# A longer chain of reciprocals, a fourth x buffer and moved transposes in a fused attention and MoE kernel

## The chip, the cores and the metric

The kernel runs on one core of one Trainium2 chip. The metric is the device time of one execution in microseconds (us); lower is better. Engines are called by the profile's names: PE is TensorE, DVE is VectorE, ACT is ScalarE, POOL is GpSimd, and SP is the engine whose queue issues the DMAs here.

## What is computed

The reference first computes a linear attention with random features and then a gated two-layer network on its output:

```python
def phi(x):                                    # x: 8 batches, 8 heads, 576 tokens, 64 wide
    proj = einsum('bhsd,df->bhsf', x, w_phi)   # 128 features
    proj = proj - max(abs(proj), axis=-1, keepdims=True)
    return concatenate([exp(proj), exp(-proj)], axis=-1)
q_p, k_p = phi(q), phi(k)
kv  = einsum('bhsf,bhsd->bhfd', k_p, v)
z   = sum(k_p, axis=2)
num = einsum('bhsf,bhfd->bhsd', q_p, kv)
den = einsum('bhsf,bhf->bhs', q_p, z)[..., None] + 1e-6
x   = (num / den).transpose(0, 2, 1, 3).reshape(4608, 512)
out = ((x @ w_a) * (x @ w_b)) @ w_out          # 512 -> 1536 -> 512
```

## The kernel before

**The attention runs in turns.** The 64 heads are handled as 32 pairs (4 pairs to a batch); pair i starts at turn 4i. A pair's steps are spread over fixed turns: `project` (q and k through `w_phi`, products `pq` and `pk`) at turn 0 of the pair, then `kv_products`, `z_products`, `kv_out` (a copy of `kv` out of PSUM), `turned_kv` (three transposes `pt` on PE, copied to `kvh` by DVE, line 274), and `num_products` (`pn`) and `den_products` (`pd`), which both need `kvh`. The table SPREAD says which turn for the first nine pairs, and PACKED for the rest; in PACKED `turned_kv` stands at turn 5, `num_products` at 7. `attention_steps` (lines 329 to 370) collects all the steps, sorts them by turn and by a fixed order inside a turn, and issues them so. The order of PE's products is fixed by that: helper `mm`, line 105, chains each to the one before. The other engines' queues are in order too; a scheduler fills them, with lists (`marks`, `acts`, `loads`) that pin some steps behind others.

**The division runs as a chain through DRAM** (`reciprocals`, lines 305 to 327), because a denominator is needed along another axis than the one it comes out of PSUM on. It has seven steps: store `den` (line 310), load it as `r` (line 313), one reciprocal on DVE (line 315), store `rec` (line 317), load it spread over the rows as `rb` (line 321, two DMAs), multiply `x` by `rb` on DVE (line 324), store `xnorm` (line 326). Each step has a turn of its own after `den_products`: REC_TURNS0 = (1, 3, 5, 6, 8, 10, 10) for pairs 0 to 4, REC_TURNS1 = (1, 3, 4, 5, 7, 8, 8) for pairs 5 and 6, REC_TURNS = (0, 1, 3, 4, 5, 6, 6) for pairs 7 to 31. All the DMAs of the chain go through SP's queue, with the loads of k, q, v and the weights.

**The network runs beside it.** Until turn 40 the attention is alone on PE, while ACT and DVE decode the network's weights (`load_weights`, lines 424 to 436, 0.8 steps a turn from turn 3, 2.2 a turn from turn 40). From turn 41 on, blocks of the network (`moe_block`, 384 tokens, six pairs of products `pa` and `pb`, then four `po`) run in between, 0.36 steps a turn for 20 turns and 0.82 a turn afterwards (line 912). The first pass covers half of the 1536 columns; `second_pass` covers the other half after the attention.

**PSUM.** Up to turn 40 the attention has all eight banks. Afterwards `ps_moe` has three banks (tag `moe`) in which `pa`, `pb`, `po`, and also `pt` and `pd`, take turns; `ps_att` has two places of two banks (tag `att`) for `pq`, `pk` and `pn`, and one bank for `kv`.

**SBUF of the chain.** `x32` (what `pn` is copied into, line 287) has three buffers, `rb` has two.

Of the kernel before, what the change touches and what calls it, by code (L numbers as in the profile page):

```python
# [9 lines left out]
F32 = mybir.dt.float32  # L10
# [8 lines left out]
P = 128  # L19
# [2 lines left out]

TURNS, ALONE, SUM_FROM = 4, 9, 15
SPREAD = dict(turned_kv=9, kv_products=5, num_products=10, z_products=6, kv_out=6, den_products=11)
PACKED = dict(summed=2, turned_kv=5, kv_products=3, num_products=7, z_products=3, kv_out=3, den_products=7)
REC_TURNS0, REC_TURNS1, REC_TURNS, X_TURNS = (1, 3, 5, 6, 8, 10, 10), (1, 3, 4, 5, 7, 8, 8), (0, 1, 3, 4, 5, 6, 6), (5, 8)
EARLY_X = (0, 2, 4)
DECODE_TURN, BLOCK_LAG = 3, 1
DECODE_ALONE, DECODE_BESIDE = 0.8, 2.2
PACE0, PACE, PACE0_TURNS = 0.36, 0.82, 21  # L30

# [13 lines left out]
def tile_kernel(ctx, tc, qP, km, kr, vm, vr, w_phi, eye, w_a, w_b, w_out, out):  # L45
# [14 lines left out]
    B, NPAIR, _, S = qP.shape  # L60
# [43 lines left out]
    def mm(out, w, x, start=True, stop=True):  # L104
        issue = lambda: nc.tensor.matmul(out, w, x, start=start, stop=stop, skip_group_check=True)  # L105
        return pe(issue) if alone else issue()
# [3 lines left out]
    def duo(name):  # L110
        if "ps" in alone:
            return alone["ps"].tile([P, 2, 512], F32, tag=f"duo{next(duos) % 3}", name=name)
        return alone["att"].tile([P, 2, 512], F32, tag="att", name=name)

    def bank(tag, name):
        if "ps" in alone:
            return alone["ps"].tile([P, 3, P], F32, tag=tag, name=name)
        if tag == "kv":
            return alone["att"].tile([P, 3, P], F32, tag="kv", bufs=1, name=name)
        return pools_moe[0].tile([P, 3, P], F32, tag="moe", name=name)  # L120

    def attention_consts(a1):
# [116 lines left out]
    def kv_products(b, pr, a1, a2, consts, st):  # L239
        e, er = st["e", b, pr], st["er", b, pr // 2]  # L240
        v32, rv = st["v", b, pr], st["rv", b, pr // 2]
        kv = st["kv", b, pr] = bank("kv", f"kv_{b}_{pr}")
        kvs = kv.rearrange("p s f -> p (s f)")
        for c in range(NFULL):
            for j in range(2):
                mm(kvs[heads[j], : 2 * F], v32[:, c, j], e[:, j, c].rearrange("p s f -> p (s f)"), start=(c == 0), stop=False)
        for j in range(2):
            mm(kvs[heads[j], : 2 * F], rv[:, pr % 2, j], er[:, j, 0].rearrange("p s f -> p (s f)"), start=False)
# [19 lines left out]
    def turned_kv(b, pr, a1, a2, consts, st):  # L268
        u = f"{b}_{pr}"
        pt = bank("pt", f"pt_{u}")  # L270
        for g in range(3):
            pe(lambda: nc.tensor.transpose(pt[:, g], st["back", b, pr][:, g], consts[1]))
        kvh = st["kvh", b, pr] = a2.tile([P, 3, P], F32, tag="kvh", bufs=1, name=f"kvh_{u}")
        nc.vector.tensor_copy(kvh, pt)  # L274

    def num_products(b, pr, a1, a2, consts, st):
        u = f"{b}_{pr}"
        kvh, eq = st["kvh", b, pr], st["eq", b, pr]
        pn = duo(f"pn_{u}")
        for t in range(2):  # L280
            for s in range(2):
                for j in range(2):
                    mm(pn[heads[j], t, :HALF], kvh[:, s, heads[j]], eq[:, j, s, times[t]], start=(s == 0), stop=(s == 1))
        i = b * NPAIR + pr
        place, bufs = (alone["early"], 2) if i in EARLY_X else (a2, 3)
        x32 = st["x", b, pr] = place.tile([P, S], F32, tag="x32", bufs=bufs, name=f"x32_{u}")
        nc.scalar.copy(x32.rearrange("p (t n) -> p t n", t=2), pn[:, :, :HALF])

    def den_products(b, pr, a1, a2, consts, st):
        u = f"{b}_{pr}"  # L290
        kvh, eq = st["kvh", b, pr], st["eq", b, pr]
        pd = bank("pt", f"pd_{u}").rearrange("p s f -> p (s f)")
        for s in range(2):
            for j in range(2):
                for t in range(2):
                    mm(pd[strips[2 * j + t], :HALF], kvh[:, 2, strips[2 * j + s]], eq[:, j, s, times[t]], start=(s == 0), stop=(s == 1))
        dn = st["dn", b, pr] = a2.tile([P, HALF], F32, tag="dn", name=f"dn_{u}")
        nc.scalar.activation(dn, pd[:, :HALF], AF.Identity, bias=consts[3])

    def behind(what, issue):  # L300

        with tc.issue_after(what[-1].ins):
            issue()

    def reciprocals(b, pr, a1, a2, st):

        n = 2 * S // P
        hs, rows = slice(2 * pr, 2 * pr + 2), slice(pr * P, (pr + 1) * P)
        one = st["dn", b, pr].rearrange("(g r) n -> g r n", r=P // 4)[:, 0]
        behind(loads, lambda: nc.sync.dma_start(den[b][hs].rearrange("h (t n) -> (h t) n", t=2), one))  # L310
        yield
        r = a2.tile([P, n], F32, tag="rec", name=f"r_{b}_{pr}")
        behind(loads, lambda: nc.sync.dma_start(r, den[b][hs].rearrange("h (a n) -> (h a) n", n=n)))
        yield
        behind(marks, lambda: nc.vector.reciprocal(r, r))
        yield
        behind(loads, lambda: nc.sync.dma_start(rec[b][hs].rearrange("h (a n) -> (h a) n", n=n), r))
        yield
        rb = a2.tile([P, S], F32, tag="rb", name=f"rb_{b}_{pr}")
        for j in range(2):  # L320
            behind(loads, lambda: nc.sync.dma_start(rb[heads[j]], rec[b][2 * pr + j : 2 * pr + j + 1].broadcast_to([D, S])))
        yield
        x32 = st["x", b, pr]
        behind(marks, lambda: nc.vector.tensor_tensor(x32, x32, rb, op=ALU.mult))
        yield
        behind(loads, lambda: nc.sync.dma_start(xnorm[b][rows], x32))
        yield

    def attention_steps(pools, consts, st):

        stages, x_first = [], first_block_x()

        def once(f, *args):
            f(*args)
            yield

        def plan(order, unit, turns):
            for t in turns:
                stages.append((t, order, len(stages), unit))

        for i in range(B * NPAIR):
            b, pr = divmod(i, NPAIR)
            t0 = TURNS * i
            args = (b, pr, *pools, consts, st)
            at = SPREAD if i < ALONE else PACKED
            if i == ALONE - 1:
                at = dict(SPREAD, turned_kv=8, num_products=8, den_products=8)
            elif i == ALONE:
                at = dict(PACKED, kv_products=4, z_products=4, kv_out=4)
            units = ((project, 0), (q_features, TURNS), (turned_kv, 0), (summed, 0), (kv_products, 0), (num_products, 0), (z_products, 0), (kv_out, 0))  # L350
            units += ((den_products, 0), (load_kq, -5), (load_v, -2 if i else 0))
            for order, (f, t) in enumerate(units):
                if f is not summed or i >= SUM_FROM:
                    plan(order, once(f, *args), [t0 + at.get(f.__name__, t)])
            rec_turns = REC_TURNS0 if i < ALONE - 4 else REC_TURNS1 if i < ALONE - 2 else REC_TURNS
            done = t0 + at["den_products"]
            plan(10, reciprocals(b, pr, *pools, st), [done + t for t in rec_turns])
            if b == 0:
                plan(11, x_first, [done + rec_turns[-1] + t for t in X_TURNS])
            if pr == NPAIR - 1:  # L360
                plan(12, b, [done + rec_turns[-1]])
        stages.sort(key=lambda x: x[:3])
        for turn_, group in itertools.groupby(stages, key=lambda x: x[0]):
            ready = None
            for *_, unit in group:
                if isinstance(unit, int):
                    ready = unit
                else:
                    next(unit, None)
            yield turn_, ready  # L370
# [142 lines left out]
    def first_block_x():  # L513

        for c in range(NCC):
            with tc.issue_after(loads[-1].ins):
                x32 = x_chunk(0, 0, c, xpool, 2)
            yield
            with tc.issue_after(acts[-1].ins), tc.issue_after(marks[-1].ins):
                x_make(0, 0, c, x32, xpool)  # L520
            yield
# [356 lines left out]
    weights, pools_moe, xpools, block_x, blocks, marks, acts, copies, loads, alone = {}, [], [xpool], {}, [0], [], [], [], [], dict(turn=0)  # L878
# [166 lines left out]
```

## Time and profile before

| | us |
|---|---|
| Median of three runs | 1198.14 |
| The three runs | 1197.65 to 1198.18 |
| The profiled execution | 1199.04 |
| Its span, first to last instruction | 1197.3 |
| PE busy | 1149.8 |
| DVE busy | 744.6 |
| ACT busy | 562.4 |

The profile is one execution, 1199.04 us long, of which 1197.3 us lie between its first and its last instruction. The page's first part gives the busy time of each engine; PE is busy for 96% of the span, so about 47 us are left in which it stands. The views by window show where in the span these lie, and the waits show what ended each.

### The profile page before, as it was taken

The page shows a single profiled execution, that of the slowest core. Times are in us where ns is not written, and L with a number is a line of the kernel's source. Part 1 is how long each engine was busy: PE and PEld are TensorE (multiplying, and loading weights), DVE is VectorE, ACT ScalarE, POOL GpSimd, SP SyncE. Part 2 cuts the span into 40 slices and gives each one's busy share as a digit, 9 for nine tenths or more (in the row PEclk, how much of TensorE's full clock was granted, in tenths as well). Part 3 has the DMA queues.
Part 4 walks back from the last instruction along what each step waited for, and adds up shares of the span by engine and source line. Part 5 has one row for each costly group of instructions (what it writes and reads, how often), then busy time and mean ns, then how long its engine had stood idle before and what let it go on. Part 6 is the DMA issues. An engine that isn't in the chain of part 4 may idle for free.

```text
span 1197.3 us, 20998 instructions
## 1 busy us (share of the span) xinstructions
PE 1149.8 (96%) x8198; PEld 1029.5 (86%) x8198; DVE 744.6 (62%) x1359; ACT 562.4 (47%) x1050; POOL 140.7 (12%) x69
## 2 busy tenths in 40 slices
PE   8997898999999999999999999999999999999998
PEld 5664676888888787879999999999999999998997
DVE  6886687554545364642999222637677695967665
ACT  6885566544454454542555222435344353435332
POOL 4443123212122121210000000000000000000000
PEclk9998999999999999999999999999999999999999
DMA  6566553314233232314886210057585777768572
GB/s 208 154 188 195 177 188 124 123 58 133 75 110 98 79 122 75 99 41 129 272 296 224 71 54 20 25 178 275 189 297 177 258 236 226 250 206 276 174 245 84
DMA packets 103075, 191.75 MB, mean 160 GB/s; under 512 B 19520, under 2 KB 54720, under 8 KB 102976
## 3 DMA queue, kind: packets, MB, share of 16 engines
q1 hardware_dynamic: 102672, 190.28, 49.3%
q8 instruction: 64, 1.05, 0.4%
q14 instruction: 35, 0.29, 0.1%
q10 hardware_dynamic: 304, 0.13, 0.0%
HBM read 150.75 MB, written 39.62 MB: 159 GB/s over the span
## 4 chain that ended last, share of the span: by engine, by line
PE 73%; DMA 11%; DVE 10%; ACT 3%; issue 2%; SPq 1%; ACTq 0%; DVEq 0%
PE pa L105 10%; PE pb L105 10%; PE po L105 10%; PE po L776 9%; PE pa L665 9%; PE pb L665 9%; PE kv L105 6%; PE pn L105 5%; PE pq L105 3%; DMA x<-xnorm 2%; PE pd L105 2%; DMA back_w<-kept_w 2%; DMA rec<-r 2%; PE pk L105 1%; DMA rb<-rec 1%
## 5 line engine op out<-in xcount | busy, mean ns | idle before, releaser
L216 POOL PARTITION_ALL_REDUCE mb<-p x64 | 140.4, 2235 | 379.9 <-ACT p L211 355.0
L105 PE MATMUL pa<-xh,w_a 128*128 128x384 f32 x576 | 162.7, 344 | 3.9 <-DVE kvh L274 3.9
L105 PE MATMUL pb<-xh,w_b 128*128 128x384 f32 x576 | 159.1, 337 | 1.3 <-ACT o L587 1.1
L105 PE MATMUL po<-hh,w_o 128*128 128x384 f32 x576 | 154.1, 340 | 1.0 <-ACT o L587 0.5
L105 PEld LDWEIGHTS pa<-xh,w_a 128*128 128x128 f32 x576 | 106.0, 189 | 11.2 <-DVE kvh L274 5.3
L105 PEld LDWEIGHTS po<-hh,w_o 128*128 128x128 f32 x576 | 104.5, 188 | 7.1 <-issue 2.5
L105 PEld LDWEIGHTS pb<-xh,w_b 128*128 128x128 f32 x576 | 105.3, 188 | 2.5 <-ACT o L587 1.7
L105 PE MATMUL po<-hl,w_o 128*128 128x384 f32 x288 | 96.8, 337 | 2.0 <-DVE hl L144 2.0
L178 DVE TENSOR_REDUCE m<-pk 128x8 f32<-128x1024 f32 x32 | 39.1, 1222 | 95.6 <-PE pk L105 95.5
L105 PE MATMUL pa<-xl,w_a 128*128 128x384 f32 x288 | 97.3, 338 | 0.0
L556 DVE TENSOR_TENSOR h<-pb,h 128x384 f32<-128x384 f32 x72 | 39.8, 552 | 91.9 <-PE pb L105 90.4
L105 PE MATMUL pb<-xl,w_b 128*128 128x384 f32 x288 | 96.8, 336 | 0.0
L105 PE MATMUL pn<-eq,kvh 128*64 128x288 f32 x512 | 71.2, 422 | 11.2 <-DVE kvh L274 11.2
L776 PE MATMUL po<-hh_s,own_o 128*128 128x384 f32 x288 | 80.5, 336 | 0.8 <-ACT u L764 0.7
L105 PEld LDWEIGHTS pn<-eq,kvh 128*64 128x64 f32 x512 | 38.6, 141 | 36.7 <-issue 14.5
L143 ACT CAST hh<-h 128x384 fp32r<-128x384 f32 x72 | 36.9, 512 | 68.9 <-DVE h L556 68.6
L105 PE MATMUL kv<-e,v 128*64 128x256 f32 x512 | 63.6, 392 | 3.3 <-ACT e L182 3.1
L587 ACT COPY o<-po 128x384 f32<-128x384 f32 x48 | 22.5, 478 | 85.2 <-PE po L105 70.2
L555 ACT COPY h<-pa 128x384 f32<-128x384 f32 x72 | 34.3, 477 | 55.2 <-PE pa L105 53.7
L776 PE MATMUL po<-hh_w,own_o 128*128 128x384 f32 x216 | 59.1, 334 | 0.0
L105 PEld LDWEIGHTS kv<-e,v 128*64 128x64 f32 x512 | 34.5, 139 | 25.5 <-issue 7.2
L105 PEld LDWEIGHTS po<-hl,w_o 128*128 128x128 f32 x288 | 54.2, 188 | 2.5 <-DVE hl L144 2.5
(257 smaller groups left out, 2641.7 us busy)
## 6 DMA issues: line engine op xcount, KB each, us to landing
back_s<-kept_s SPq DMA_DIRECT2D x71, 512.0 KB, 4.1
back_w<-kept_w SPq DMA_DIRECT2D x52, 512.0 KB, 4.9
q<-in_qP SPq DMA_DIRECT2D x32, 288.0 KB, 3.9
rb<-rec SPq DMA_DIRECT2D x64, 144.0 KB, 3.2
xnorm<-x SPq DMA_DIRECT2D x32, 288.0 KB, 2.5
part<-o SPq DMA_DIRECT2D x48, 192.0 KB, 1.9
o<-part SPq DMA_DIRECT2D x24, 384.0 KB, 5.2
out_x<-o SPq DMA_DIRECT2D x48, 192.0 KB, 1.9
```

Source lines behind the costliest of these rows:

```text
L105: issue = lambda: nc.tensor.matmul(out, w, x, start=start, stop=stop, skip_group_check=True)
L143: (eng_hi.copy if eng_hi is nc.scalar else eng_hi.tensor_copy)(hi, src)
L178: nc.vector.tensor_reduce(out=m, in_=p, op=ALU.max, axis=AX.X, apply_absolute_value=True)
L216: nc.gpsimd.partition_all_reduce(mb, p32[:, j], P, bass_isa.ReduceOp.absmax)
L555: nc.scalar.copy(h32, pab["a"])
L556: nc.vector.tensor_tensor(h32, pab["b"], h32, op=ALU.mult)
L587: nc.scalar.copy(o, acc)
L665: in_turn(lambda: nc.tensor.matmul(acc[to][i], w_, x_, skip_group_check=True, **at), u.startswith("1_0"))
L776: in_turn(lambda: nc.tensor.matmul(acc[m, to], w_, h_, skip_group_check=True, **f), False)
```

## The change

It does five things. `turned_kv` moves from turn 5 to turn 6 of a pair in PACKED. After turn 40 its tile `pt` takes a place of `att` (two banks) instead of one of the three `moe` banks; `pd` stays in a `moe` bank. The chain of reciprocals gets the ten-turn table REC_TURNS0 for all pairs of batches 0 to 6, and the six-turn table stays for the last batch. `x32` gets a fourth buffer, and `rb` is left with one. Decoding starts at turn 5 instead of 3.

```diff
-PACKED = dict(summed=2, turned_kv=5, kv_products=3, num_products=7, z_products=3, kv_out=3, den_products=7)
-REC_TURNS0, REC_TURNS1, REC_TURNS, X_TURNS = (1, 3, 5, 6, 8, 10, 10), (1, 3, 4, 5, 7, 8, 8), (0, 1, 3, 4, 5, 6, 6), (5, 8)
+PACKED = dict(summed=2, turned_kv=6, kv_products=3, num_products=7, z_products=3, kv_out=3, den_products=7)
+REC_TURNS0, REC_TURNS, X_TURNS = (1, 3, 5, 6, 8, 10, 10), (0, 1, 3, 4, 5, 6, 6), (5, 8)
...
-DECODE_TURN, BLOCK_LAG = 3, 1
+DECODE_TURN, BLOCK_LAG = 5, 1
...
         if tag == "kv":
             return alone["att"].tile([P, 3, P], F32, tag="kv", bufs=1, name=name)
+        if tag == "pt":
+            return alone["att"].tile([P, 2, 512], F32, tag="att", name=name)[:, 0, : 3 * P].rearrange("p (s f) -> p s f", s=3)
         return pools_moe[0].tile([P, 3, P], F32, tag="moe", name=name)
...
-        place, bufs = (alone["early"], 2) if i in EARLY_X else (a2, 3)
+        place, bufs = (alone["early"], 2) if i in EARLY_X else (a2, 4)
...
-        pd = bank("pt", f"pd_{u}").rearrange("p s f -> p (s f)")
+        pd = bank("pt" if "ps" in alone else "pd", f"pd_{u}").rearrange("p s f -> p (s f)")
...
-        rb = a2.tile([P, S], F32, tag="rb", name=f"rb_{b}_{pr}")
+        rb = a2.tile([P, S], F32, tag="rb", bufs=1, name=f"rb_{b}_{pr}")
...
-            rec_turns = REC_TURNS0 if i < ALONE - 4 else REC_TURNS1 if i < ALONE - 2 else REC_TURNS
+            rec_turns = REC_TURNS0 if b < B - 1 else REC_TURNS
```

## Rows read from the trace of the kernel before

**Rows 1.** The page, part 1: busy us, share of the span, instructions of each engine.
```profile
PE 1149.8 (96%) x8198; PEld 1029.5 (86%) x8198; DVE 744.6 (62%) x1359; ACT 562.4 (47%) x1050; POOL 140.7 (12%) x69
```

**Rows 2.** Busy time by window: length, PE, PEld, DVE, ACT, POOL, granted clock, DMA share, GB/s.
```profile
97.00:123.00 26.00, 18.57 (x223) 11.50 (x220) 17.05 (x28) 11.69 (x18) 4.57 (x2) 0.87 0.65 197
123.00:135.00 12.00, 8.95 (x59) 8.02 (x60) 5.35 (x9) 5.76 (x10) 1.54 (x1) 0.93 0.42 133
196.00:207.00 11.00, 8.24 (x51) 6.05 (x53) 8.94 (x12) 5.14 (x6) 4.26 (x2) 0.84 0.37 119
207.00:540.00 333.00, 326.29 (x2524) 268.76 (x2520) 168.58 (x253) 161.45 (x263) 68.85 (x32) 1.00 0.30 92
```

**Rows 3.** Waits of PE, whole span: who waited for whom, total us, times, longest.
```profile
PE pn L105 <- DVE kvh L274: 11.2, 5, 6.8
PE pq L105 <- ACT p L199: 6.3, 9, 3.1
PE pa L105 <- DVE kvh L274: 3.9, 6, 0.7
```

**Rows 4.** PE in order of time: start, us, what, idle before it and its releaser.
```profile
23.58 3.57 PE L105 MATMUL pn<-eq,kvh 128*64 128x288 f32 x16 [2.66 <-DVE kvh L274]
109.04 4.06 PE L105 MATMUL pn<-eq,kvh 128*64 128x288 f32 x16 [6.81 <-DVE kvh L274]
118.61 2.11 PE L105 MATMUL pn<-eq,kvh 128*64 128x288 f32 x16
131.92 0.76 PE L105 MATMUL pq<-q,w 64*128 64x288 f32 x4 [3.06 <-ACT p L199]
168.12 0.45 PE L105 MATMUL pa<-xh,w_a 128*128 128x384 f32 x1 [0.65 <-DVE kvh L274]
202.36 3.27 PE L105 MATMUL kv<-e,v 128*64 128x256 f32 x16 [2.76 <-ACT e L182]
```

**Rows 5.** Busy time by window, behind four of these waits (columns as in rows 2).
```profile
22.00:28.00 6.00, 4.42 (x44) 2.70 (x48) 5.93 (x9) 4.05 (x7) 3.28 (x2) 0.72 0.59 216
109.00:114.00 5.00, 4.96 (x52) 2.87 (x56) 2.84 (x7) 3.90 (x8) 0.00 (x0) 0.61 0.69 185
132.00:137.00 5.00, 5.00 (x22) 4.62 (x23) 4.97 (x6) 4.28 (x5) 3.54 (x2) 0.66 0.39 113
203.00:207.00 4.00, 4.00 (x30) 2.32 (x28) 3.28 (x5) 0.00 (x0) 0.00 (x0) 0.74 0.32 112
```

**Rows 6.** DVE in order of time, from 96 to 127 us.
```profile
96.11 0.76 DVE L324 TENSOR_TENSOR x<-x,rb 128x576 f32<-128x576 f32 x1 [3.45 <-DMA rb<-rec]
100.50 0.76 DVE L324 TENSOR_TENSOR x<-x,rb 128x576 f32<-128x576 f32 x1 [3.64 <-DMA rb<-rec]
...
108.35 0.55 DVE L274 COPY kvh<-pt 128x384 f32<-128x384 f32 x1
...
126.84 0.22 DVE L315 RECIPROCAL r<-r 128x9 f32<-128x9 f32 x1 [6.91 <-DMA r<-den]
```

**Rows 7.** The chain that ended last: start, us, what.
```profile
86.91 4.13 DMA rec<-r
...
96.72 3.69 DMA rb<-rec
...
122.85 3.96 DMA r<-den
```

**Rows 8.** DVE in order of time ahead of the wait at 23.58.
```profile
18.29 1.68 DVE L432 SCALAR_TENSOR_TENSOR w_a<-raw_a,w_a 128x512 f32<-128x512 uint32 x1
19.88 0.69 DVE L433 TENSOR_TENSOR w_a<-w_a 128x512 f32<-128x512 f32 x1
```

**Rows 9.** DVE, then PE, in order of time: the narrowest of pairs 10 to 31.
```profile
485.02 0.56 DVE L274 COPY kvh<-pt 128x384 f32<-128x384 f32 x1 [0.87 <-PE pt L272]
...
488.03 1.95 PE L105 MATMUL kv<-e,v 128*64 128x256 f32 x16
...
490.24 2.11 PE L105 MATMUL pn<-eq,kvh 128*64 128x288 f32 x16
```

## Prediction, written before the result was known

> **What bounds the kernel now.** I read the page first. PE is busy for 1149.8 of 1197.3 us [rows 1], so no more than 47 us can be had by taking waits away, and the question is which of them the change reaches. The views by window come next: from 207 to 540 us, where the network runs beside the attention, PE is busy for 326.29 of 333 us at full granted clock, while three short stretches are much worse, 18.57 of 26, 8.95 of 12 and 8.24 of 11 us [rows 2]. The waits of PE name who ended them [rows 3], and the order of time gives them places [rows 4]. The reader should see that the large waits of the attention are few: 6.81 us before 109.04, 3.06 before 131.92, 2.76 before 202.36 and 2.66 before 23.58. Behind each of these the granted clock is 0.61, 0.66, 0.74 and 0.72 of the full 2.4 GHz for 5, 5, 4 and 6 us, that is a mix of the 1.2 and the 2.4 GHz level [rows 5]; the same sixteen `pn` take 4.06 us at 109.04 and 2.11 us at 118.61 [rows 4]. So a wait costs its length and a tail behind it.
>
> **Why PE waited there.** DVE shows it [rows 6]. At 96.11 and at 100.50 its queue stood 3.45 and 3.64 us in front of a product of line 324 until `rb` had landed; the features of the next pair and the copy `kvh` stood behind, and `kvh` came at 108.35. At 126.84 the reciprocal of line 315 held DVE for 6.91 us until `r` had landed, with it the decoding, which passes between DVE and ACT, and ACT's copy for which `pq` waits stood behind that [rows 4]. The chain that ended last gives the prices of the hops through DRAM: 4.13 us for `rec`, 3.69 for `rb`, 3.96 for `r` [rows 7]. So DVE reaches the steps of the division before their data, and queues in order hand that on to PE.
>
> **Part 1, ten turns.** For pairs 5 to 8 the reciprocal and the product move one to four turns later, behind the features and the `kvh` that now stand behind them. Reciprocal: the 6.91 us at 126.84 go, and with them PE's 3.06 us and the tail behind, 5 x (1 - 0.66) = 1.7: 4.8 us, taken whole. Product: of the two waits ahead of 108.35 only the second belongs to a pair that changes (pair 5); the first is pair 4's, which has ten turns already and still waited 3.45 us. So `kvh` comes earlier by the wait and the product itself, 3.64 + 0.76 = 4.4 us, not 6.81, and I count 1.0 of the tail of 5 x 0.39 = 1.95, since some 2.4 us of wait stay: 5.4 us, between 0 and 8.8. The wait of 2.76 us at 202.36 was ended by ACT's exponential `e`, which needs DVE's features [rows 4]; whether the division or only the decoding made these late isn't plain, so I take half of 2.76 + 4 x 0.26 = 3.8: 1.9 us, between 0 and 3.8. Later on DVE is busy for half the time only (168.58 of 333 us) [rows 2] and a turn more or less moves nothing. `x` comes four turns later for batches 1 to 6. By the pace in the code (line 912) a block of the network takes about 13 turns, and counting steps by turn, every block starts at the same turn as before: its input was waiting. That costs nothing; if a block did starve, the same products would run after the attention.
>
> **Part 2, transposes.** `pa` waited six times for `kvh`, 3.9 us in all, 0.65 us each [rows 3, 4], because `pt` holds one of the three banks. With `pt` among the attention's places that wait has no cause left; what stays is that `att` gets a fifth tenant, and the tile whose place it takes, `pk` of two turns earlier, has been read by then, and the one that takes its place, the next pair's first `pq`, comes behind `pn`, which needs `kvh` anyway. I count 3.0 of the 3.9 us, between 0 and 3.9. The later turn costs cover: before, DVE finished `kvh` at least 4.66 us ahead of `pn` (485.02 + 0.56 to 490.24) [rows 9], in 22 pairs. By the pace, in 7 of the 23 pairs from pair 9 on no products of the network run in turn 6, and then only the `kv` products, 490.24 - 488.03 = 2.2 us, lie between the transposes and `pn` [rows 9], less the 0.56 us of the copy. Idle DVE makes that in time; DVE behind one decoding or feature step of 0.7 to 1.7 us [rows 8] doesn't. I charge 7 x 0.4 = 2.8 us, between 0 and the price of the second rival below.
>
> **Part 3, decoding two turns later.** The wait at 23.58 has the decoding steps of 1.68 and 0.69 us standing in DVE ahead of the features [rows 8]. Counted in turns, these two steps fall behind the features of pair 2 in the change, so 2.4 us of 2.66 go, and part of the tail 6 x 0.28 = 1.7, in which the wait itself lies: I take 3.0 us, between 0 and 4.4. The same work comes two turns later at turn 40, 1.6 steps more beside the network, on a DVE that has room.
>
> **Part 4, buffers.** The fourth `x32` only matches the longer life of `x`. `rb` loses its second buffer: the load of pair i + 1 then waits, at the head of SP's queue, for the product of pair i, and everything that SP issues stands behind, the next loads of k, q and v among it. Products of neighbours lie four turns apart, loads two turns ahead of their product, so this mostly costs nothing. At two places the chains close up: pairs 7 and 8 (products at turns 49 and 50), and pairs 27 and 28 (both at turn 125, since the last batch keeps six turns). There DVE can stand 3.69 us, an `rb` [rows 7], between the products. I charge 1.0 us in all, between 0 and 7.4, because PE has the products of a turn or two to do meanwhile.
>
> The Trainium skill (Trainium Kernel Development and Optimization, Best Practices) says to double-buffer so that transfers overlap with compute, which speaks against this edit; the trace has a second buffer and shows no wait for one, so no run here bears it out yet.
>
> **The sum.** Gains: 4.8 + 5.4 + 1.9 + 3.0 + 3.0 = 18.1 us. Costs: 2.8 + 1.0 = 3.8 us. Net 14.3 us against the profiled execution's 1199.04 (a span of 1197.3 and 1.7 us around it): 1184.7. The median is 0.9 us below that execution, so 1183.8 us. With all gains at their upper ends, 4.8 + 8.8 + 3.8 + 3.9 + 4.4 = 25.7 us, and no costs, the median would be 1172.4.
>
> **Rivals.** First, ten turns don't suffice. For it speaks the product at 96.11: pair 4 had ten turns and still held DVE for 3.45 us [rows 6]. Then pairs 5 to 8 wait as pair 4 did, the 5.4 and the 1.9 us are lost, and PE's 4.8 us halve: 18.1 - 9.7 - 3.8 = 4.6 us, 1193.5. Against it: pair 4's `rec` and `rb` stood in SP's queue among those of a shorter chain. Second, the slower side: `kvh` comes too late for `pn`, pair after pair. In the first nine pairs only the `kv` products stand between transposes and `pn`, and there `pn` waited 11.2 us in all [rows 3], 1.24 us a pair. If the later turn made the 22 pairs beside the network like that, it would cost 22 x 1.24 = 27 us: 18.1 - 1.0 - 27 = -9.9, so 1208. It decides from 17.1 / 22 = 0.8 us a pair on. Against it: a DVE half idle there, and products of the network in turn 6 of 16 of the 23 pairs. Third, the single `rb` buffer costs PE its 7.4 us: 18.1 - 2.8 - 7.4 = 7.9 us, 1190.2. Fourth, no change: DVE and ACT are so full between 97 and 207 us that each wait taken away is replaced by the next engine's; then only the 3.0 us of the transposes stay, less costs of 0 to 3.8: 1195 to 1199. Fifth, everything comes at its upper end: 1172 to 1176.
>
> **How the numbers follow.** The forecast (1177 to 1190) gets 0.50, the first rival 0.18, the second 0.13, the third 0.05, the fourth 0.07, the fifth 0.07. The likeliest gives 1183.8. The range reaches from the upper end of all gains, 1172, to the middle of the fourth rival, 1197.5, and leaves out the second rival and half of the fourth. About 0.2%, 2.4 us, is what a measurement can tell here from no change. Faster takes the forecast, the first, third and fifth rivals, nearly whole: 0.79; the same 0.08; slower 0.13.
>
> **What would show it.** Right: DVE's idle time before lines 324 and 315 between 90 and 140 us falls from 14.0 us [rows 6] to pair 4's 3 to 4; `pn` of pair 8 waits 2 to 3 us in place of 6.81; the wait of `pq` over 3 us is gone, and the clock stays at 1.00 after it; no `pa` waits for `kvh`; the wait at 23.58 is under 1 us. Wrong: `pn` waiting for `kvh` beyond 207 us in more than the 7 pairs named, a line 324 that waits for `rb` near turns 50 and 125 with PE idle behind it, or new waits of `kv` for ACT's `e` where the old ones have gone.

## The result, and the profile after

| | before | after |
|---|---|---|
| Median, six runs of each on one chip, us | 1198.18 | 1184.92 |
| These runs, us | 1197.65 to 1200.32 | 1179.69 to 1189.18 |
| The profiled execution, us | 1199.04 | 1189.18 |
| Its span, us, and mean granted clock | 1197.3, 0.993 | 1187.4, 0.989 |

The ratio of after to before is 0.9883, with a 95% interval of 0.9854 to 0.9911. The forecast was 1183.8 us. One thing is to be kept in mind for what follows: the profiled execution is the slowest of the six, and the six differ mostly as their clock does (1179.69 us at a mean granted clock of 0.998, 1181.33 at 0.996, 1189.18 at 0.989). In the changed kernel all lines from 122 on are higher by 2 (also in the trials that keep the transposes' new place; the others have the numbers of before): the copy `kvh` is line 276, the reciprocal 317, the load of `rb` 323, the product 326, ACT's copy `p` 201.

The engines do the same work as before [rows 1], as the page's first part shows (busy us, share of the span, instructions):

```profile
PE 1150.9 (97%) x8198; PEld 1033.5 (87%) x8198; DVE 737.1 (62%) x1359; ACT 561.9 (47%) x1050; POOL 140.3 (12%) x69
```

So the ten microseconds are waits. Busy time by window of after (length, PE, PEld, DVE, ACT, POOL, granted clock, DMA share, GB/s) answers to [rows 2] and to the first of [rows 5]:

```profile
22.00:28.00 6.00, 5.13 (x88) 3.55 (x87) 5.86 (x8) 5.28 (x10) 3.56 (x2) 1.00 0.30 96
97.00:123.00 26.00, 21.86 (x238) 16.67 (x239) 16.58 (x30) 14.63 (x24) 6.19 (x4) 1.00 0.67 204
123.00:135.00 12.00, 12.00 (x139) 8.89 (x138) 10.59 (x18) 7.73 (x14) 2.15 (x2) 1.00 0.60 188
196.00:207.00 11.00, 11.00 (x95) 9.21 (x92) 4.61 (x7) 5.84 (x9) 2.47 (x2) 1.00 0.33 108
...
149.30:155.00 5.70, 5.70 (x18) 4.95 (x19) 4.45 (x8) 3.23 (x5) 1.94 (x1) 0.50 0.70 215
186.30:192.00 5.70, 5.70 (x25) 4.82 (x25) 4.54 (x6) 4.36 (x5) 3.63 (x2) 0.72 0.40 117
```

Of the three bad stretches two are full now (12.00 of 12, 11.00 of 11 us), and in the first PE stands 4.1 us instead of 7.4 (21.86 of 26 us). All three have the full clock, and so has the one behind 22 us. But two new bad stretches have appeared, behind 149 and 186 us, with clocks of 0.50 and 0.72. The waits of PE over the whole span (who waited for whom, total us, times, longest) answer to [rows 3]:

```profile
PE pq L105 <- ACT p L201: 8.1, 8, 3.6
PE pt L274 <- ACT dn L300: 3.3, 3, 2.2
PE pn L105 <- DVE kvh L276: 3.0, 4, 1.1
```

`pn` waits 3.0 instead of 11.2 us, and `pa` for `kvh` not at all; `pq` waits longer than before, 8.1 instead of 6.3. In the order of time of PE (start, us, what, the wait before it and its releaser; it answers to [rows 4]) these are:

```profile
98.02 2.16 PE L105 MATMUL pn<-eq,kvh 128*64 128x288 f32 x16 [1.12 <-DVE kvh L276]
...
117.69 0.76 PE L105 MATMUL pq<-q,w 64*128 64x288 f32 x4 [0.21 <-ACT p L201]
...
149.25 1.33 PE L105 MATMUL pq<-q,w 64*128 64x288 f32 x4 [3.59 <-ACT p L201]
...
186.26 1.33 PE L105 MATMUL pq<-q,w 64*128 64x288 f32 x4 [2.84 <-ACT p L201]
...
192.34 1.95 PE L105 MATMUL kv<-e,v 128*64 128x256 f32 x16 [0.18 <-ACT e L184]
...
534.73 2.16 PE L105 MATMUL pn<-eq,kvh 128*64 128x288 f32 x16 [0.30 <-DVE kvh L276]
```

The wait of 6.81 us has become 1.12, the one of 2.76 us (`kv` of pair 15) 0.18, and the one of 3.06 us (the second `pq` of pair 11) 0.21. Two other waits are long instead: 3.59 us at 149.25, before the second `pq` of pair 13, and 2.84 us at 186.26, before that of pair 15. DVE and SP show where the first comes from. DVE in order of time, the products of pairs 4 and 5, then 7 and 8 (it answers to [rows 6]):

```profile
90.32 0.76 DVE L326 TENSOR_TENSOR x<-x,rb 128x576 f32<-128x576 f32 x1 [3.34 <-DMA rb<-rec]
...
101.21 0.76 DVE L326 TENSOR_TENSOR x<-x,rb 128x576 f32<-128x576 f32 x1 [1.88 <-DMA rb<-rec]
...
135.36 0.76 DVE L326 TENSOR_TENSOR x<-x,rb 128x576 f32<-128x576 f32 x1
...
141.97 0.76 DVE L326 TENSOR_TENSOR x<-x,rb 128x576 f32<-128x576 f32 x1 [2.73 <-DMA rb<-rec]
```

SP's queue in order of time, the loads of `rb` of pairs 7 and 8:

```profile
126.25 1.13 SPq L323 DMA_DIRECT2D rb<-rec  x2
...
138.13 1.10 SPq L323 DMA_DIRECT2D rb<-rec  x2
```

The load of pair 8 was issued at 138.13, only after the product of pair 7 (to 136.12) had given the single buffer back, and its data came for the product at 141.97. Decoding stood behind that product in DVE, and behind the decoding ACT's copy `p`, for which `pq` waited. This is the third rival's mechanism at the place that the prediction named, turns 49 and 50.

Where the time was won is best read from when `pn` of certain pairs ended (us from the span's start, read from PE in order of time):

| End of `pn` of pair | 0 | 7 | 9 | 12 | 15 | 31 |
|---|---|---|---|---|---|---|
| before | 27.1 | 95.0 | 120.7 | 176.8 | 226.1 | 548.8 |
| after | 22.2 | 89.3 | 109.3 | 165.9 | 214.8 | 536.9 |
| after is ahead by | 4.9 | 5.7 | 11.4 | 10.9 | 11.3 | 11.9 |

In this execution 4.9 us come at the first pair, 5.7 more between pairs 7 and 9, and nearly nothing afterwards: what the wait at 131.92 and the `pa` gave, the new waits at 149.25 and 186.26 with their slow clocks took. Of the 11.9 us 2.0 are lost again behind pair 31: the rest of the span takes 650.5 us against 648.5 before. Over the fourteen profiled executions of this document that rest takes 643.7 to 650.5 us, whether or not the kernel has the change, so 2 us there say nothing about an edit.

### The profile page after: what moved, and what is told of

Its sections match the earlier page's. It is cut to its first block, busy times and chain, and to the rows that moved or that the text cites. A ratio compares the mean times of both kernels' runs of the same rounds, so it can differ in the third digit from the quotient of the medians.

```text
span 1187.4 us, 21021 instructions
## 1 busy us (share of the span) xinstructions
PE 1150.9 (97%) x8198; PEld 1033.5 (87%) x8198; DVE 737.1 (62%) x1359; ACT 561.9 (47%) x1050; POOL 140.3 (12%) x69
## 4 chain that ended last, share of the span: by engine, by line
PE 76%; DVE 10%; DMA 7%; ACT 4%; issue 2%; SPq 1%; DVEq 0%; ACTq 0%
PE pa L105 11%; PE pb L105 10%; PE po L778 10%; PE po L105 10%; PE pa L667 9%; PE pb L667 9%; PE kv L105 6%; PE pn L105 4%; PE pq L105 3%; PE pd L105 2%; DMA x<-xnorm 2%; PE pk L105 1%; DMA rb<-rec 1%; DMA back_w<-kept_w 1%; DMA raw_a<-in_w_a 1%
## 5 line engine op out<-in xcount | busy, mean ns | idle before, releaser
L105 PE MATMUL pn<-eq,kvh 128*64 128x288 f32 x512 | 68.3, 409 | 3.1 <-DVE kvh L276 3.0
L105 PE MATMUL pq<-q,w 64*128 64x288 f32 x256 | 49.0, 456 | 8.1 <-ACT p L201 8.1
```

## The experiments

The change has three parts that can be made alone: the chain (ten turns, with four `x32` and one `rb`), the place and turn of the transposes, and the later decoding. Theory: the chain brings most of it, the decoding some 3 us, the transposes about nothing, and the parts add as in the prediction's sum. The rivals: another part brings the time, or the parts don't add, since each wait removed is replaced by the next engine's. Twelve kernels were timed in three groups, each on one chip with the kernel before, whose median there was 1195.28, 1195.68 and 1195.67 us. The column "us" is the ratio's distance from 1 times 1195.5; a ratio's interval is about 2 to 4 us to either side.

| Kernel | median us (runs) | ratio to before [95%] | us |
|---|---|---|---|
| before again (e12) | 1195.03 (10) | 0.9989 [0.9967, 1.0011] | -1.3 |
| chain alone (e3) | 1194.45 (12) | 0.9994 [0.9970, 1.0018] | -0.7 |
| decoding alone (e10) | 1197.13 (12) | 1.0006 [0.9984, 1.0029] | +0.7 |
| transposes alone (e4) | 1191.23 (12) | 0.9968 [0.9949, 0.9987] | -3.8 |
| chain and decoding (e2) | 1186.02 (7) | 0.9932 [0.9904, 0.9960] | -8.1 |
| chain and transposes (e1) | 1190.33 (12) | 0.9950 [0.9926, 0.9974] | -6.0 |
| transposes and decoding (e11) | 1187.16 (9) | 0.9928 [0.9905, 0.9951] | -8.6 |
| all, the changed kernel (e0) | 1185.05 (6) | 0.9903 [0.9869, 0.9937] | -11.6 |
| all, transposes one turn earlier (e8) | 1191.81 (12) | 0.9965 [0.9946, 0.9984] | -4.2 |
| all, shorter chain of pair 7 (e6) | 1183.06 (7) | 0.9906 [0.9877, 0.9935] | -11.2 |
| e6, faster decoding (e13) | 1184.35 (6) | 0.9895 [0.9874, 0.9915] | -12.6 |
| e6, decoding one turn later still (e14) | 1185.11 (6) | 0.9908 [0.9890, 0.9927] | -11.0 |

**How far one execution can be trusted: e0 and e12.** Both repeat a kernel unchanged.

> The changed kernel itself, beside the other three on one chip. Expected from its first measurement: 0.988 of the kernel before, about 1182 where that is 1195. If the runs' spread follows the granted clock, time less 1190 us times (1 - clock) stays within 2 us from run to run.

> The kernel before once more, with a profile of its own. The prediction rested on one execution of it, in which DVE stood 3.45, 3.64 and 6.91 us for rb and r between 90 and 127 us and PE 6.81 and 3.06 us behind. Theory: these waits are of that execution's DMA landings and vary; in another execution PE's waits of pn and pq there sum to 3 to 7 us instead of 9.9, which is why the chain alone gained 0.8 us and not 11. Rival: they are the same within 1 us, and the chain's gain is lost again further on. Time: 1195 to 1198.

The changed kernel gave 1185.05 us, as the first time (1184.92), and not the 1182 expected. Less 1190 us times (1 - clock), its six executions lie within 2.7 us (1176.0 to 1178.7), a little more than the 2 expected, against 10.6 us as measured: most of the spread goes with the clock. Its profiled execution, of 1183.1 us, is one of clock 0.994. The kernel before, profiled again (1197.79 us), has the wait of `pn` again but a shorter one of `pq`; PE in order of time of e12:

```profile
108.32 3.94 PE L105 MATMUL pn<-eq,kvh 128*64 128x288 f32 x16 [6.13 <-DVE kvh L274]
...
129.90 0.76 PE L105 MATMUL pq<-q,w 64*128 64x288 f32 x4 [1.60 <-ACT p L199]
```

Together 7.7 us, against 6.81 + 3.06 = 9.9 [rows 4]. Neither expectation (3 to 7, or the same within 1) meets that: the places stay, the sizes vary by some 2 us. The prediction's terms were taken from one execution, so each carries an error of that kind.

**The chain alone: e3.**

```diff
-REC_TURNS0, REC_TURNS1, REC_TURNS, X_TURNS = (1, 3, 5, 6, 8, 10, 10), (1, 3, 4, 5, 7, 8, 8), (0, 1, 3, 4, 5, 6, 6), (5, 8)
+REC_TURNS0, REC_TURNS, X_TURNS = (1, 3, 5, 6, 8, 10, 10), (0, 1, 3, 4, 5, 6, 6), (5, 8)
-        place, bufs = (alone["early"], 2) if i in EARLY_X else (a2, 3)
+        place, bufs = (alone["early"], 2) if i in EARLY_X else (a2, 4)
-        rb = a2.tile([P, S], F32, tag="rb", name=f"rb_{b}_{pr}")
+        rb = a2.tile([P, S], F32, tag="rb", bufs=1, name=f"rb_{b}_{pr}")
-            rec_turns = REC_TURNS0 if i < ALONE - 4 else REC_TURNS1 if i < ALONE - 2 else REC_TURNS
+            rec_turns = REC_TURNS0 if b < B - 1 else REC_TURNS
```

> The kernel before with the chain alone: ten turns for batches 0 to 6, four x buffers, one rb buffer; transposes and decoding as before. Theory (the sum's part 1 and 4): 4.8 + 5.4 + 1.9 - 1.0 = 11 us faster than before, about 1187; DVE's wait of 6.91 us before line 315 at 126.84 and PE's waits of 6.81 and 3.06 us are gone. Rival: without the other parts a wait of 3 to 4 us for the single rb buffer or for the decoding takes their place, so that only half is gained: 1192 or more.

The median moved by 0.8 us, within the interval, so of the two expectations the rival's (1192 or more) holds. The trace shows a part of the mechanism at work all the same; PE in order of time of e3:

```profile
101.96 2.16 PE L105 MATMUL pn<-eq,kvh 128*64 128x288 f32 x16 [1.39 <-DVE kvh L274]
...
122.23 0.76 PE L105 MATMUL pq<-q,w 64*128 64x288 f32 x4 [2.35 <-ACT p L199]
...
152.84 0.76 PE L105 MATMUL pq<-q,w 64*128 64x288 f32 x4 [1.84 <-ACT p L199]
...
193.25 3.49 PE L105 MATMUL kv<-e,v 128*64 128x256 f32 x16 [2.77 <-ACT e L182]
```

The 6.81 us have become 1.39, no `pq` waits more than 2.4 us, and `pn` of pair 9 ends at 111.7 us, of pair 31 at 540.2 (e12: 120.2 and 547.4). Between pairs 7 and 9 that is 6.9 us, where the prediction had 5.4 for the product's wait, in this execution: 1191.94 us, at clock 0.996. The twelve executions run from 1187.63 us (0.998) to 1202.10 us (0.990), and their mean clock is that of the kernel before on the same chip (0.9936 and 0.9937). The profiled one is 2.6 us under their mean, and its clock alone is worth 1190 x (0.996 - 0.9936) = 2.9 us (an estimate), so a good part of its lead is that of an execution with little slow clock. What stands in the other eleven no trace here shows: that stays open.

The `pq` of pair 11, at 131.92 before, for which the prediction gave the chain 4.8 us, still waits 2.35 us at 122.23, although no reciprocal holds DVE any more. ACT in order of time of e3 shows what stands there instead:

```profile
117.95 0.67 ACT L424 ACTIVATE w_b<-raw_b 128x512 f32<-128x512 f32 x1 [5.04 <-DMA raw_b<-in_w_b]
...
121.55 0.63 ACT L199 COPY p<-pq 128x576 f32<-128x576 f32 x1
```

A decoding step waits 5.04 us for its raw weights, and the copy `p` comes behind it. The wait at 193.25 also stands where it was, so of the 1.9 us that the prediction took for it the chain brings none.

**The decoding alone: e10.**

```diff
-DECODE_TURN, BLOCK_LAG = 3, 1
+DECODE_TURN, BLOCK_LAG = 5, 1
```

> The kernel before with one part alone: decoding starts at turn 5. Theory of the prediction: the wait of pn at 23.58 us (2.66 us) and its tail go, 3 us. Rival, from undoing it (1190.3 against about 1184): it is worth 5 to 8 us, because it also moves the places where decoding steps stand in front of features and copies later on, so PE's waits between 97 and 207 us shrink as well. So 0.997 of the time before by the first, 0.994 by the second.

The wait at 23.58 is gone (`pn` of pair 0 ends at 22.3 instead of 27.1 us), but at pair 9 only 2.6 us of the 4.8 are left (118.1 against 120.7), and the median shows nothing, neither the 0.997 nor the 0.994 expected. DVE, then PE, in order of time of e10, show where it went:

```profile
108.51 0.22 DVE L315 RECIPROCAL r<-r 128x9 f32<-128x9 f32 x1 [4.13 <-DMA r<-den]
...
122.51 0.22 DVE L315 RECIPROCAL r<-r 128x9 f32<-128x9 f32 x1 [5.46 <-DMA r<-den]
```

```profile
99.16 0.55 PE L272 MATMUL pt<-ident,back 128*128 128x128 f32 x3 [3.13 <-ACT dn L298]
...
111.93 0.90 PE L272 MATMUL pt<-ident,back 128*128 128x128 f32 x3 [4.43 <-ACT dn L298]
...
126.42 0.76 PE L105 MATMUL pq<-q,w 64*128 64x288 f32 x4 [0.21 <-ACT p L199]
```

PE arrives earlier at the short chain, DVE stands in front of the reciprocal until `r` has landed, decoding and ACT's copies wait behind it, and with them the transposes, 7.6 us in all between 80 and 210 us, where before these waited 2.0 us. The short chain takes back what the later decoding gave. The other kernel with the short chain and this decoding, e11, has 8.1 us of these waits; with the long chain (after, e0, e2, e6, e8) they are 1.2 to 3.0 us. The last line tells more: the reciprocal at 122.51 held DVE for 5.46 us, and the `pq` of pair 11 behind it waits only 0.21, because no decoding step stands between it and ACT's copy there.

The executions also have less clock: 0.9912 in the mean of the twelve, against 0.9937 in the 26 of the kernel before on this chip. By 1190 us times the difference that is 3.1 us (an estimate), without which this part would be 2.6 us faster than before.

**The transposes alone: e4.**

```diff
-PACKED = dict(summed=2, turned_kv=5, ...)
+PACKED = dict(summed=2, turned_kv=6, ...)
+        if tag == "pt":
+            return alone["att"].tile([P, 2, 512], F32, tag="att", name=name)[:, 0, : 3 * P].rearrange("p (s f) -> p s f", s=3)
-        pd = bank("pt", f"pd_{u}").rearrange("p s f -> p (s f)")
+        pd = bank("pt" if "ps" in alone else "pd", f"pd_{u}").rearrange("p s f -> p (s f)")
```

> The kernel before with one part alone: turned_kv at turn 6 and pt in the attention's places. Theory of the prediction: 3.0 us gained, 2.8 lost, so the same within 2 us. From the runs so far: each of the other two parts alone changed the time by -0.8 and +1.4 us, and each pair of parts by -5 to -9. If the parts only work together, this one alone is within 2 us of before as well; if it is the part that carries the gain, it is 5 us faster or more.

The one part that is faster by itself, by 3.8 us, which lies between the two expectations. The long wait is untouched; PE in order of time of e4:

```profile
108.48 4.11 PE L105 MATMUL pn<-eq,kvh 128*64 128x288 f32 x16 [7.08 <-DVE kvh L276]
```

Pair 9 ends as before (120.3 against 120.7 us); the gain comes by pair 12 (173.0 against 176.8) and in the waits of `pa`, of which none is left (542.7 against 548.8 at pair 31). The prediction's part 2, 3.0 us less 2.8 for lost cover, had this at nearly nothing.

**Each part taken out of the whole: e2, e1, e11.** Without the transposes:

```diff
-PACKED = dict(summed=2, turned_kv=6, ...)
+PACKED = dict(summed=2, turned_kv=5, ...)
-        if tag == "pt":
-            return alone["att"].tile([P, 2, 512], F32, tag="att", name=name)[:, 0, : 3 * P].rearrange("p (s f) -> p s f", s=3)
```

> The changed kernel with the transposes as before: turned_kv at turn 5 and pt in one of the three moe banks. Theory (the sum's part 2: 3.0 us gained, 2.8 us lost): within 2 us of 1184.9; pa waits for kvh six times or so again, 0.65 us each, 3.9 us in all. Rival: the lost cover cost nothing (the changed kernel shows pn waiting 0.30 us once beyond 207 us), so undoing this costs the whole 3.9 us: about 1189.

The waits of `pa` come back in full, as the waits of PE of e2 show (total us, times, longest):

```profile
PE pa L105 <- DVE kvh L274: 3.9, 6, 0.7
```

The median lies 1.0 us above e0's; by the ratios it is 3.5 us, and the intervals overlap, so the times decide for neither expectation. Without the later decoding:

```diff
-DECODE_TURN, BLOCK_LAG = 5, 1
+DECODE_TURN, BLOCK_LAG = 3, 1
```

> The changed kernel with one part undone: decoding starts at turn 3 again. Theory (the sum's part 3): the wait of pn for kvh before 23.58 us comes back, 2.66 us, with its tail of slow clock, so the time is 3 to 4 us over the changed kernel's 1184.9: about 1188. Rival: the start only hands the decoding on to the stretch from 100 to 200 us, where DVE and ACT are full, so undoing it costs 3 us at 23 us and gives 2 to 4 us back later: 1183 to 1186, with the waits of pq for ACT's copy (8.1 us in all in the changed kernel) falling below 5 us.

This cost 5.3 us by the medians, 5.6 by the ratios, more than the 3 to 4 expected. PE in order of time of e1:

```profile
22.52 3.68 PE L105 MATMUL pn<-eq,kvh 128*64 128x288 f32 x16 [2.53 <-DVE kvh L276]
...
122.93 1.33 PE L105 MATMUL pq<-q,w 64*128 64x288 f32 x4 [4.48 <-ACT p L201]
```

The wait at the start is back with its price, 22.2 to 26.2 us at pair 0. The rival fails: the waits of `pq` sum to 9.6 us, where it said less than 5. One of them, 4.48 us at 122.93, is that of pair 11 again, with the ten-turn chain and no reciprocal in front of DVE; as in e3, ACT stood for `raw_b` ahead of it (5.67 us). All profiled executions together settle which part this wait belongs to: where decoding starts at turn 3 (before, e12, e4, e3, e1) it is 3.06, 1.60, 0.41, 2.35 and 4.48 us, and where it starts at turn 5 or 6 it is 0.21 in each of the nine, with either chain. So the turn of the decoding is felt a hundred microseconds later too.

Without the longer chain (the old tables and their choice, three `x32`, two `rb`):

```diff
-        place, bufs = (alone["early"], 2) if i in EARLY_X else (a2, 4)
+        place, bufs = (alone["early"], 2) if i in EARLY_X else (a2, 3)
-        rb = a2.tile([P, S], F32, tag="rb", bufs=1, name=f"rb_{b}_{pr}")
+        rb = a2.tile([P, S], F32, tag="rb", name=f"rb_{b}_{pr}")
-            rec_turns = REC_TURNS0 if b < B - 1 else REC_TURNS
+            rec_turns = REC_TURNS0 if i < ALONE - 4 else REC_TURNS1 if i < ALONE - 2 else REC_TURNS
```

> The changed kernel with the chain undone: the three tables of before, three x buffers, two rb buffers; transposes and decoding as changed. Theory of the prediction: the chain was worth 11 us, so this is 11 us over the changed kernel, and DVE waits 3 to 7 us for r and rb before its lines 317 and 326 between 90 and 130 us, with PE's waits of pn and pq behind them. Rival, from the chain alone, which gained 0.8 us on a chip: the chain is worth 0 to 3 us here as well, since PE's next wait stands right behind the one removed.

Only 2.1 us were lost by the medians, 3.0 by the ratios: the rival that the chain is not what brings the time held. The trace has the same waits as e10's; PE in order of time of e11:

```profile
112.57 0.90 PE L274 MATMUL pt<-ident,back 128*128 128x128 f32 x3 [4.10 <-ACT dn L300]
```

DVE stood 13.1 us in front of the reciprocal between 60 and 160 us. Pair 9 ends at 120.0 us, 10.7 later than in after, pair 31 at 540.5, only 3.6 later.

**The single `rb` buffer: e6.** A second buffer beside the four `x32` wasn't tried. The same wait was removed by giving pair 7 the eight-turn chain, so that its product comes three turns ahead of pair 8's instead of one, and a turn ahead of pair 8's load.

```diff
-            rec_turns = REC_TURNS0 if b < B - 1 else REC_TURNS
+            rec_turns = (1, 3, 4, 5, 7, 8, 8) if i == ALONE - 2 else REC_TURNS0 if b < B - 1 else REC_TURNS
```

> The changed kernel, but pair 7 takes the eight-turn chain (1, 3, 4, 5, 7, 8, 8), so that its product comes at turn 47, ahead of pair 8's load of rb at turn 48; nothing else differs. Theory: in the changed kernel the wait of pq at 149.25 us (3.59 us, then the clock at 0.50 for 5.7 us, 2.9 us more) comes from DVE standing 2.73 us before pair 8's product, because its rb could only be loaded once pair 7's product had freed the one rb buffer. With the clash gone the wait falls below 1 us and the clock stays at 1.00 behind it: 4 to 6 us less in a profile that has the slow stretch, 1180 to 1182 in the median, and a narrower spread. Rival: DVE and ACT are full of decoding there, so PE waits as long for the same copy whether rb is in time or not: 1184 to 1186.

SP's queue in order of time, the `rb` of pair 8, and then PE's, of e6:

```profile
127.11 1.09 SPq L323 DMA_DIRECT2D rb<-rec  x2
```

```profile
146.97 0.76 PE L105 MATMUL pq<-q,w 64*128 64x288 f32 x4 [0.47 <-ACT p L201]
...
181.57 1.33 PE L105 MATMUL pq<-q,w 64*128 64x288 f32 x4 [2.62 <-ACT p L201]
```

The load goes out 11 us earlier, the wait of 3.59 us has become 0.47, and the clock from 147 to 153 us is 1.00. The other executions agree on this `pq` of pair 13: it waits 1.84 to 3.59 us in the six with the long chain for pair 7 and one `rb` (after, e0, e3, e2, e1, e8), 0.46 or 0.47 in the three with pair 7's eight turns (e6, e13, e14), and under 1 us in the five with the short chain and two `rb`. So its cause is shown. Its price isn't: the median is 2.0 us below e0's and misses the 1180 to 1182 expected, the ratios are alike (0.9906 and 0.9903), and e0's own execution waited 2.04 us at that place, not 3.59. At turn 125, where pairs 27 and 28 close up, DVE stood 3.63 us before its product at 511.33 in after, and no wait of PE followed. The Trainium skill (Trainium Kernel Development and Optimization, Best Practices) says to double-buffer so that transfers overlap with compute. Here the trace agrees at one of some thirty places, the one where two uses of the buffer are a turn apart and DVE is full; at the others no wait of PE was traced to the buffer.

**Whether the transposes need the later turn: e8.** All of the change, with the transposes at turn 5.

```diff
-PACKED = dict(summed=2, turned_kv=6, ...)
+PACKED = dict(summed=2, turned_kv=5, ...)
```

> The changed kernel with turned_kv at turn 5 again, but pt still in the attention's places: it parts the turn from the place. Theory: the place took away the six waits of pa for kvh (3.9 us) and the later turn only cost cover, so this is as fast as the changed kernel or 1 to 2 us faster, with no wait of pa. Rival: the later turn is what helps, since kvh no longer stands behind the features in DVE's queue; then this is 2 to 4 us slower than the changed kernel.

It was 7.4 us slower than the whole by the ratios, more than either expectation, and 3.9 slower than e2, which has the old place with the same turn. From the waits of PE of e8 (total us, times, longest), then PE in order of time, the first of the five:

```profile
PE pt L274 <- DVE d L181: 8.9, 5, 1.9
```

```profile
133.56 0.52 PE L274 MATMUL pt<-ident,back 128*128 128x128 f32 x3 [1.79 <-DVE d L181]
```

At turn 5 `pt` takes the place of a `pk` that DVE's features are still reading. So the two edits of part 2 belong together, and the turn later, which the prediction counted as a cost alone, is what makes the place worth having. What the later turn would do in the old place wasn't run.

**Two further trials: e13 and e14**, both on e6: the decoding at 2.6 steps a turn beside the network, and the decoding begun at turn 6.

```diff
-DECODE_ALONE, DECODE_BESIDE = 0.8, 2.2
+DECODE_ALONE, DECODE_BESIDE = 0.8, 2.6
```

> The changed kernel with pair 7's eight-turn chain, and decoding at 2.6 steps a turn instead of 2.2 beside the network. Theory: the wait of pq for ACT's copy near 181 us (2.62 us, then slow clock) comes from DVE doing the last decoding steps and four lines 146 of the next block's x at once; with the decoding over two turns earlier it goes, 3 to 4 us less than the same kernel with 2.2 (0.9906 of before), about 0.987. Rival: DVE and ACT are just as full from 105 to 150 us, and the wait only moves there: no gain or 2 us lost.

```diff
-DECODE_TURN, BLOCK_LAG = 5, 1
+DECODE_TURN, BLOCK_LAG = 6, 1
```

> The changed kernel with pair 7's eight-turn chain, and decoding from turn 6 instead of 5. If a later start only has to put the first decoding steps behind the features of pair 2, a turn more changes nothing within 2 us: 0.99 of before, no wait of pn at 23 us. If what counts is where the decoding steps fall among the pairs' steps later on, the time moves by 3 us or more either way, with PE's waits between 85 and 190 us at other places.

Neither is faster than the changed kernel by more than the intervals allow (0.9895 and 0.9908 against 0.9903): the rival held for e13, and for e14 the expectation of no change. In both the waits moved. PE in order of time of e13, then of e14:

```profile
106.79 0.90 PE L274 MATMUL pt<-ident,back 128*128 128x128 f32 x3 [5.33 <-ACT dn L300]
```

```profile
111.29 0.90 PE L274 MATMUL pt<-ident,back 128*128 128x128 f32 x3 [5.02 <-ACT dn L300]
...
189.57 0.76 PE L105 MATMUL pq<-q,w 64*128 64x288 f32 x4 [2.39 <-ACT p L201]
```

e13 has lost e6's wait at 181.57 and got 5.33 us at 106.79, where e6 had 2.97 (at 104.43).

## Why the prediction was right, and where it was not

The total was right, 1183.8 against 1184.92, and so was the sign; the division among the parts was not. It put some 11 us on the chain, 3.0 on the decoding and 0.2 on the transposes. Alone these gave -0.7, +0.7 and -3.8 us; as the last part added to the other two, by the ratios, -3.0, -5.6 and -3.5.

**What failed is the sum, and the booking of two of its terms.** The sum adds terms that were read from one trace as if each wait removed stayed removed. The parts alone sum to 3.8 us, together they make 11.6. The error of the three added is about 4.6 us and that of the whole 4.1 (from the intervals' half widths), so the gap of 7.8 is wider than the 6.1 that these make together, though not by much. Some 3 us of the gap are the low clock of the executions of the decoding alone: with 1190 us times (1 - clock) taken off each execution (an estimate), the parts gain 0.5, 2.6 and 3.8 us and the whole 11.4, a gap of 4.5 with an error of about 3.

The traces show how the parts meet. Between 85 and 200 us DVE and ACT are two queues in order that pass work between them: features, decoding, division, copies for PE. A part removes what stands in front at one place, and PE then arrives earlier at the next. With the decoding alone that is the reciprocal of the short chain (4.13 and 5.46 us), and the transposes wait 7.6 us. With the long chain and the early decoding it is the decoding step in ACT (5.04 us in e3, 5.67 in e1), and the `pq` of pair 11 waits. With both neither stands there, but the waits at 149.25 and 186.26 do. One reading doesn't bear out the gap: at `pn` of pair 31 the profiled executions of the chain, the decoding and the transposes alone lead the mean of the two of before (548.1 us) by 7.9, 2.0 and 5.4 us, 15.3 in all, and the two of the whole by 11.2 and 17.2. So how much the parts fall short of the whole rests on the times, and only where they meet rests on the traces. The fourth rival said of the whole that each wait is replaced by the next. It holds, within the error, of the chain and of the decoding by themselves, and not of the three together. The prediction gave it 0.07 and never asked it of the parts.

**The product's wait** (5.4 us, 0 to 8.8). Right in the profile: `pn` waits 1.12 us at 98.02, a little less than the 2 to 3 forecast, the clock behind is 1.00, and 5.7 us are won between pairs 7 and 9. DVE's idle time before lines 326 and 317 fell from 14.0 (16.1 with the 2.13 us at 111.82, which [rows 6] leave out) to 3.34 + 1.88 = 5.2 us, where 3 to 4 were forecast; the 2.73 us at 141.97 stand just behind. Pair 4's wait stayed, as the prediction had assumed. In the times of e3 and e11 much less of it is seen, 0.7 to 3.0 us for the whole chain.

**The reciprocal's wait** (4.8 us, "taken whole"). DVE's wait went with the long chain, but PE's wait wasn't the reciprocal's. The `pq` of pair 11 waits 2.35 and 4.48 us in e3 and e1, where no reciprocal holds DVE, and 0.21 in e10, where one holds it for 5.46. What counts is the decoding step between the two, so the term belongs to the later decoding. It was also read from a large case: behind 6.91, 4.83 and 4.28 us of DVE (before, e12, e4) PE lost 3.06, 1.60 and 0.41.

**The single `rb`** (1.0 us, 0 to 7.4). In the profiled execution of after 3.59 us and 5.7 x (1 - 0.50) = 2.9 of slow clock stand at 149.25. That term was mis-sized: 1.0 us charged, 6.4 paid in this execution at one of the two places named, nothing at the other; in the medians of e6 it is 2 us at most, with an interval of about 3.5 to either side. So two of the prediction's signs of being right failed here: a wait of `pq` over 3 us is back, and the clock behind it isn't 1.00.

**The wait of `kv`** (1.9 us). It is gone in after (0.18 at 192.34), and this too is the decoding's doing: it is 2.26 to 2.77 us in the five executions that decode from turn 3, with either chain, and at most 1.14 in the nine others. But nothing is won by it. The `pq` of the same pair waits 0.91 to 1.00 us in the five, and in the nine 1.77 to 2.91 (2.84 at 186.26 in after); only in e13, with the faster decoding, is that wait gone.

**The transposes** (3.0 of 3.9, less 2.8). The gain came whole: no `pa` waits in after or e4, and all 3.9 us return in e2. The charge was the mis-sized term. Beyond 207 us `pn` waited for `kvh` once, 0.30 us; the second rival (0.8 us a pair) never came near. Its price was too high as well: 6.81 of its 11.2 us are the wait of pair 8, which the prediction itself put down to the product. DVE half idle made `kvh` in time.

**The decoding** (3.0 of 4.4). The wait at 23.58 went whole with its tail: pair 0 is 4.9 us ahead, more than the upper end of 4.4. What was left out is that the same turn decides what stands before `pq` of pair 11 and `kv` of pair 15: taking it out of the whole costs 5.6 us.

So one term too high (the chain, which had the decoding's waits booked to it) was balanced by two too low (the transposes and the decoding). The good total is in part luck.

## What to carry to other kernels

Read a change of several edits as a chain of covers: before terms are added, ask of each edit what PE meets next if this edit alone is made, and whether another edit removes that. Where two queues in order feed the bounding engine, edits that give nothing alone can give 8 us together, as the chain and the decoding did, so a part that measures "no change" isn't to be dropped on that alone. Before a wait is booked to one edit, look at it in every kernel that has the edit and in every one that hasn't: here that moved two terms from the chain to the decoding. A buffer that is freed and filled again a turn apart is the place to look for when a second buffer is saved.

## What the hardware showed that was not expected

The same kernel's executions differ by 10 us, and by the mean granted clock: the changed kernel's second set runs from 1177.75 us at 1.000 to 1188.35 at 0.991. It isn't fixed which wait is followed by a slow clock. Busy time by window behind the wait of `pq` near 181 us, first of e6 (2.62 us waited), then of e0 (2.84 us waited, at 181.27):

```profile
181.50:188.00 6.50, 6.43 (x20) 5.67 (x21) 4.65 (x7) 4.66 (x6) 4.33 (x2) 0.50 0.42 135
```

```profile
181.20:187.00 5.80, 4.66 (x27) 3.92 (x29) 5.12 (x9) 4.95 (x7) 4.20 (x2) 1.00 0.43 138
```

Behind the shorter wait the clock was at half of 2.4 GHz for 6.5 us, behind the longer one it was full. A tail behind a wait is thus something that may come, worth some 3 us each time (6.5 x 0.5), and the prediction counted one behind every large wait.
